# Weight preparation moved from fills into visits, and eight late stores on another queue: attention followed by a SiLU layer on one core

## The chip, the core and the metric

The kernel runs on one core of a Trainium2 chip. A core has four computing engines, each with an instruction queue of its own that it works through in order: TensorE (PE, with its weight loads shown as PEld), VectorE (DVE), ScalarE (ACT) and GpSimd (POOL). SyncE (SP) computes nothing here; it issues most of the DMA transfers between the chip's main memory (HBM) and the core's memory (SBUF). Matrix products land in PSUM, which has few buffers, and some other engine must empty them. The metric is the device time of one execution in microseconds. Before the change its median is 1379.21 us over 10 runs, from 1376.03 to 1383.0.

## What is computed

```
q_n, k_n = rmsnorm(q, g_q), rmsnorm(k, g_k)         # q, k, v: (8, 12, 448, 64)
attn     = softmax(q_n @ k_n.T / sqrt(64))
x        = (attn @ v) as (8 * 448, 12 * 64)         # 3584 rows of 768
h        = x @ w_in                                 # w_in: (768, 2048)
out      = (h * sigmoid(h)) @ w_out                 # w_out: (2048, 768)
```

The inputs q, k and v are 32-bit floats; w_in and w_out come as 64-bit floats, so the kernel rounds them to 32 bits itself.

## The kernel before

**Visits and fills.** The attention part runs over 24 visits, c = 0 to 23: a visit treats four heads of one batch, and three visits finish a batch. `visit(c)` (L1212) computes the scores of c on PE (L579), takes their exponentials on ACT (L584), weighs the values on PE (L611), divides the sums of the visit before on VectorE (`divide`, L669), and at its end adds exponentials on VectorE (`add`, L625). After each visit stands `between(c)` (L1267): it transposes the queries and keys of the next visit, sums the exponentials, takes reciprocals on VectorE (L654) and spreads them by DMA (`spread`, L660 and L662).

**The fill.** Inside `between`, `fill` (L1155) is called twice. It runs matrix work of the first layer for batches that are already finished: from c = 6 on, two batches per group of six visits (`GROUP` is 6). That work is `halves_in`: for each of eight blocks, seven products of a fast multiplication scheme (the class `Seven`), each of three steps on PE (L745; a step shows as two matmul records). A product needs a PSUM buffer, of which there are two during this part, and VectorE or ACT must empty it (L704, L752, L758). In the first group a call of `fill` has 13 steps. Small pieces of work for other engines, the list `others`, are dealt out evenly among these steps: with n others, the k-th is issued when n * steps // 13 reaches k. The list `prompt` (the two reciprocals) is dealt first: one at the start, one at step 3.

**Preparing w_in.** The weights come in 24 pieces, six for each of four chunks, handled by a `Rounder`. `load` issues the DMA from SP (L75). `open` splits the words by two activations on ACT (L90, L91). `round` takes three instructions on VectorE (L113, L116, L120), one addition on GpSimd (L124), and then tries to issue two further loads, which can only go where an earlier piece of the same buffer has been rounded. When a chunk is rounded, `sum_w_in(chunk, step)` makes four sums of its quarters on VectorE (L701, L704, 768 columns each), which the products need as left operands.

Twelve pieces and the sums of chunk 0 are done beside c = 0 to 5. The others are placed by hand. `weights_in(c, half)` (L1200) returns the pieces and sums for one call of `fill`; with i = 2 * (c - 6) + half, the table `pieces_at` says how many pieces are rounded and the next ones opened there, and `sums_at` which sums are made.

**The second layer.** After the visits, `quad(q)` runs for q = 0 to 6 over 512 rows of the output each, again with the fast scheme, on two levels. `results[i, j]` holds the two tiles (128 rows by 384 columns each) of the upper (i = 1) or lower (i = 2) rows and the left (j = 1) or right (j = 2) columns. `save_out(q, i, j)` (L1075) stores them by `store` (L442), which cuts a tile where the order of the output's rows asks for it and issues each piece at L451 from SP unless other queues are named. In the last quad the final product is stored by quarters, on the queues of ACT and SP in turn (L1135 to L1139).

**After all of it** the engines meet at closing semaphores (L1543).

Of the kernel before, what the change touches and what calls it, by code (L numbers as in the profile page):

```python
# [441 lines left out]
def store(nc, out, z, column, o, m0, *queues):  # L442


    at, queues = 0, queues or [nc.sync]
    while at < o.shape[0]:
        b, c = divmod(column + at, z.S)
        j, p = divmod(c, z.R)
        n = min(z.R - p, o.shape[0] - at)
        rows = out[ds(b * z.S, z.S), ds(m0, o.shape[1])].rearrange("(p j) m -> j p m", j=z.J)  # L450
        queues[0].dma_start(rows[j, ds(p, n)], o[ds(at, n), :])  # L451
        queues = queues[1:] + queues[:1]
        at += n
# [3 lines left out]
def bounded(  # L457
# [3 lines left out]
    P, D, R, J, S = z.P, z.D, z.R, z.J, z.S  # L461
# [9 lines left out]
    GROUP = z.NPAIR  # L471
# [10 lines left out]
    work = mem.tile([P, 16 * S + z.NK], F32, name="work")  # L482
    at = 0

    def piece(n):
        nonlocal at
        at += n
        return work[:, at - n : at]
# [6 lines left out]
    r = [piece(S) for _ in range(2)]  # L495
# [37 lines left out]
    def x_of(c, i):  # L533
        b, cp = divmod(c, z.NPAIR // 2)
        return xT(b, 2 * cp + i)
# [34 lines left out]
    def scores(c, j, i=None):  # L570


        two = ps.tile([P, 2, BANK], F32, name="sc", bufs=2)
        for half in range(2):
            pair = half if j == LEFT else i
            keys = kT[:, ds((z.KA, z.KB)[0 if j == LEFT else i] + j * P, P)]
            for h in range(2):
                rows = ds(h * D, D)
                nc.tensor.matmul(  # L579
                    two[ds(half * D, D), h, 0:S], keys[rows, ts(half, D)], qT[rows, pair, :],  # L580
                    start=True, stop=True,
                )
        for h in range(2):
            nc.scalar.activation(  # L584
                eleft[:, h] if j == LEFT else weights(c, j)[:, i, h], two[:, h, 0:S], AF.Exp,
                scale=norm.column(c, i, h, j),
            )
# [28 lines left out]
    def add(c, j):  # L616

        def one(i):
            total = weights(c, 0)[:, i]
            if j == LEFT:  # L620
                rows = ds(i * D, D)
                total, more = total[rows], eleft[rows]
            else:
                more = weights(c, j)[:, i]
            nc.vector.tensor_tensor(out=total, in0=total, in1=more, op=ALU.add)  # L625

        return [lambda: one(0), lambda: one(1)]
# [38 lines left out]
    def divide(c, source):  # L666
        for i in range(2):
            x = x_of(c, i)
            nc.vector.tensor_tensor(  # L669
                out=x, in0=x if source is None else source[i], in1=r[i], op=ALU.mult  # L670
            )

    def normalise(c):


        if c >= NC:
            return []

        def piece(name, i):
            t = scratch[i if c < GROUP + 2 else 0]  # L680
            source = raw_q[c % 2] if c < GROUP else q_of(c)
            if name == "q":
                norm.squares_q(c, source, t, i)
            else:
                norm.squares_k(c, place[f"k{c % 2}"], t, i)
            if name == "q" and c < GROUP:
                norm.root(c, name, i)
                norm.scale(c, source, q_of(c), i, nc.gpsimd)
                if i == 1 and c + 2 < GROUP:
                    load_q(c + 2)  # L690
            elif i == 1:
                norm.root(c, name)
                if name == "q":
                    for m in range(2):
                        norm.scale(c, source, q_of(c), m, nc.gpsimd)

        return [lambda a=a: piece(*a) for a in (("q", 0), ("q", 1), ("k", 0), ("k", 1))]
# [8 lines left out]
    def left_sums(a11, a12, a21, a22, s1, s2, s4, steps=range(4)):  # L706

        for step in steps:
            (
                lambda: plus(a21, a22, s1),  # L710
                lambda: minus(s1, a11, s2),
                lambda: minus(a11, a21, a21),
                lambda: minus(a12, s2, s4),
            )[step]()

    def right_sums(b11, b12, b21, b22, t1, t2, t4):

        minus(b12, b11, t1)
        minus(b22, t1, t2)
        minus(b22, b12, b12)  # L720
        minus(b21, t2, t4)
# [70 lines left out]
    def sum_w_in(i, step):  # L792

        assert room.w_in.rounded >= (i + 1) * z.NW
        summed.add((i, step))
        w = room.chunk(i).rearrange("p (c m r k) -> p c m r k", c=z.NW, m=2, r=2)
        up, low = w[:, 0:HW], w[:, HW:]
        s = room.sums(i).rearrange("p (s c m k) -> p s c m k", s=3, c=HW, m=2)
        left_sums(
            up[:, :, :, 0], low[:, :, :, 0], up[:, :, :, 1], low[:, :, :, 1],  # L800
            s[:, 0], s[:, 1], s[:, 2], (step,),
        )

    def quarters(group, c):

        return [xT(b, c + up) for up in (0, HW) for b in group]

    def sums_of_x(c):
        return [sums_x[:, ts(i * HW + c, S)] for i in range(3)]

    def sum_x(group, c):
        right_sums(*quarters(group, c), *sums_of_x(c))
# [119 lines left out]
    QUADS = NT // 4  # L932
# [8 lines left out]
    def take(n, *which):  # L941

        for i in which or range(len(regions)):
            a, at = regions[i]
            if at + n <= a.shape[1]:
                regions[i][1] += n
                return a[:, ds(at, n)]
        raise AssertionError
# [8 lines left out]
    results = {(1, 1): [take(z.HALF, i) for i in (7, 5)]}  # L957
    copies = [take(QUARTER, i) for i in (0, 0, 1, 2)]
    for at in ((1, 2), (2, 1), (2, 2)):
        a = take(2 * z.HALF)  # L960
        results[at] = [a[:, ts(t, z.HALF)] for t in range(2)]
    a = take(2 * z.HALF)
# [109 lines left out]
            )  # L1072
        return o

    def save_out(q, i, j, tiles=range(2)):  # L1075
        for t in tiles:
            store(
                nc, out, z, (4 * q + 2 * (i - 1) + t) * P, results[i, j][t], (j - 1) * z.HALF
            )

    def quad(q):
# [109 lines left out]

    pieces_at = {0: 1, 1: 1, 2: 1, 3: 2, 4: 1, 5: 1, 6: 2, 7: 2, 8: 1}
    sums_at = {-6: [(0, 0)], -5: [(0, 1)], -4: [(0, 2)], -3: [(0, 3)]}
    for i, chunk in ((1, 1), (5, 2), (8, 3)):
        sums_at[i] = [(chunk, 0), (chunk, 1)]
        sums_at.setdefault(i if i == 5 else i + 1, []).extend([(chunk, 2), (chunk, 3)])

    def weights_in(c, half):  # L1200
        def piece():
            room.w_in.round()
            room.w_in.open()

        i = 2 * (c - GROUP) + half
        work = [piece] * (1 if c < GROUP else pieces_at.get(i, 0))
        return work + [lambda a=a: sum_w_in(*a) for a in sums_at.get(i, ())]

    def last_two(c):
        return [c // GROUP * 2 - 2, c // GROUP * 2 - 1]  # L1210

    def visit(c):  # L1212

        beside = normalise(c + 1) if c <= GROUP else []
        if c < NC:
            scores(c, 0, 0)
        run_all(beside[0:1])
        if c > 0:
            weigh(c - 1, LEFT)
            weigh(c - 1, LEFT - 1, 0)  # L1220
        if c < NC:
            scores(c, 0, 1)
        if not 0 < c < GROUP:
            run_all(beside[1:2])
        if c > 0:
            weigh(c - 1, LEFT - 1, 1)
            if c - 1 < EARLY:
                for i in range(2):
                    nc.vector.tensor_copy(x_of(c - 1, i), sums[i])
                if inverting:  # L1230
                    if c > 1:
                        divide(c - 2, None)
                    run_all(inverting)
                    inverting.clear()
            else:
                divide(c - 1, sums)
                if c < NC and c % GROUP == 0:
                    for i in range(0 if c == GROUP else 1, HW):
                        sum_x(last_two(c), i)
            if c < GROUP:  # L1240
                run_all(beside[1:2])
            if c + 1 < NC:
                loads["vrest"](c + 1)
        if c == NC:
            return
        scores(c, 1, 0)
        scores(c, 1, 1)
        if c < GROUP:
            run_all(beside[2:3])
        weigh(c, 0, 1)  # L1250
        scores(c, 2, 0)
        if c < GROUP:
            run_all(beside[3:4])
        weigh(c, 1, 1)
        scores(c, 2, 1)
        weigh(c, 0, 0)
        run_all(add(c, 1))
        weigh(c, 1, 0)
        scores(c, LEFT)
        if c + 1 < NC:  # L1260
            loads["v"](c + 1)

    def run_all(work):
        for piece in work:
            piece()
# [282 lines left out]
```

## Time and profile before

| what | value |
|---|---|
| median of 10 runs | 1379.21 us |
| the profiled execution, its own time | 1378.12 us |
| its span, from the first instruction to the last | 1376.3 us |
| VectorE's part in rounding w_in, one piece: L113, L116, L120 (median of each where nothing disturbs it) | 0.42, 0.43, 0.69 us |
| a w_in sum (L701, median) | 0.95 us |
| GpSimd's addition of one piece (L124, median) | 1.29 us |
| a reciprocal, half of the columns (L654) | 1.55 us |
| the first group, c = 6 to 11 | from 134.39 to 355.00 us |
| the last instructions on VectorE and the last stores' issues | 1371.3 to 1372.1 us |

A row of the profile's timeline gives the start, the duration, the engine, the source line and operation, the tiles as "written <- read", the shapes and a count where equal rows are merged. In square brackets stands the idle time before it and what ended that. "SPq" and "ACTq" mark DMA issues. A table by stage gives, for a stretch from A to B, its length and then each engine's busy time with its number of instructions.

### The profile page before, as it was taken

The numbers are of one execution on the slowest core, as the hardware profiler recorded it, in microseconds if no ns is written. First come the engines' busy times: TensorE is split into PE (matmuls) and PEld (weight loads), VectorE is DVE, ScalarE is ACT, GpSimd is POOL, SyncE is SP. The second block draws the span as 40 slices with busy tenths as digits, with TensorE's granted clock in tenths as the row PEclk, the third lists the DMA queues.
The fourth block names the chain that finished last, engine by engine and source line by source line (L and its number), as shares of the span: only waits on it lengthen the run. The fifth ranks groups of instructions, "written<-read, shape, count | busy, mean of one in ns | idle before, by whom it ended". The sixth has DMA issues, their size and how long they took to land.

```text
span 1376.3 us, 19392 instructions
## 1 busy us (share of the span) xinstructions
PE 1335.1 (97%) x7185; PEld 817.8 (59%) x7185; DVE 888.3 (65%) x1497; ACT 517.9 (38%) x882; POOL 338.3 (25%) x233
## 2 busy tenths in 40 slices
PE   7998999999999999999999999999999999999998
PEld 4333444444444444444444455555998989898988
DVE  3887976665644544644543677667876676777775
ACT  6875555655545544545554244420000000000000
POOL 4774443332332233223320144420000000000000
PEclk9999999999999999999999999999999999999999
DMA  7654444323222322322221248421423232322321
GB/s 181 187 156 103 112 129 139 98 78 98 77 71 77 105 78 77 105 78 73 69 86 41 98 141 270 163 96 43 126 73 96 74 96 73 101 83 92 105 65 37
DMA packets 175692, 139.40 MB, mean 101 GB/s; under 512 B 104036, under 2 KB 159716, under 8 KB 175588
## 3 DMA queue, kind: packets, MB, share of 16 engines
q1 hardware_dynamic: 175264, 137.86, 34.1%
q8 instruction: 59, 0.97, 0.3%
q14 instruction: 45, 0.37, 0.1%
q10 hardware_dynamic: 324, 0.20, 0.1%
HBM read 88.47 MB, written 41.29 MB: 94 GB/s over the span
## 4 chain that ended last, share of the span: by engine, by line
PE 88%; DVE 6%; ACT 2%; issue 2%; SPq 1%; DMA 0%; POOL 0%; DVEq 0%; ACTq 0%
PE mm L745 27%; PE alone L1037 25%; PE av L611 9%; PE mm L1069 8%; PE sc L579 8%; PE alone L745 7%; DVE work L654 2%; PE sc L546 1%; PE sc L561 1%; PE sc L645 1%; PE mm L645 1%; ACT work L584 1%; DVE work L625 1%; DVE rms L396 1%; DVE W L116 1%
## 5 line engine op out<-in xcount | busy, mean ns | idle before, releaser
L745 PE MATMUL mm<-x,W 128*128 128x448 f32 x636 | 255.9, 546 | 10.7 <-DVE stage L704 7.4
L584 ACT ACTIVATE work<-sc,rms 128x448 f32<-128x448 f32 x324 | 184.3, 632 | 85.8 <-PE sc L579 77.4
L424 POOL TENSOR_TENSOR rms<-rms,minus_half 128x14 f32<-128x14 f32 (+4 forms) x55 | 138.5, 2521 | 250.4 <-DVE rms L420 194.8
L745 PEld LDWEIGHTS mm<-x,W 128*128 128x128 f32 x636 | 118.2, 191 | 134.1 <-issue 105.9
L745 PE MATMUL mm<-sums_x,W 128*128 128x448 f32 x456 | 183.4, 542 | 2.3 <-DVE stage L704 1.5
L625 DVE TENSOR_TENSOR work<-work 128x896 f32<-128x896 f32 (+1 forms) x114 | 123.4, 1116 | 77.2 <-ACT work L584 75.2
L579 PE MATMUL sc<-work 64*64 64x448 f32 x1344 | 164.3, 546 | 6.5 <-ACT work L584 4.7
L611 PE MATMUL av<-work,rows 64*64 64x448 f32 x1296 | 153.5, 547 | 7.8 <-issue 2.4
L745 PEld LDWEIGHTS mm<-sums_x,W 128*128 128x128 f32 x456 | 85.2, 190 | 88.4 <-issue 79.6
L611 PEld LDWEIGHTS av<-work,rows 64*64 64x64 f32 x1296 | 51.8, 133 | 95.8 <-issue 85.7
L579 PEld LDWEIGHTS sc<-work 64*64 64x64 f32 x1344 | 52.2, 133 | 88.8 <-issue 35.9
L1037 PE MATMUL alone<-W,rows 128*128 128x192 f32 x552 | 103.1, 326 | 0.0
L396 DVE TENSOR_REDUCE rms<-squares 112x8 f32<-112x512 f32 (+1 forms) x80 | 52.4, 655 | 64.3 <-ACT squares L395 63.4
L1037 PEld LDWEIGHTS alone<-W,rows 128*128 128x128 f32 x552 | 92.0, 190 | 0.0
L1069 PE MATMUL mm<-W,work 128*128 128x384 f32 x264 | 88.7, 486 | 0.0
L1037 PE MATMUL alone<-W,work 128*128 128x192 f32 x468 | 88.2, 326 | 0.0
L760 POOL TENSOR_TENSOR parts<-parts,stage 128x448 f32<-128x448 f32 x31 | 42.6, 1373 | 168.2 <-DVE parts L704 168.1
L1037 PEld LDWEIGHTS alone<-W,work 128*128 128x128 f32 x468 | 78.1, 190 | 0.0
L1047 ACT COPY work<-alone 128x192 f32<-128x192 f32 x38 | 12.1, 319 | 165.4 <-PE alone L1037 138.1
L1069 PEld LDWEIGHTS mm<-W,work 128*128 128x128 f32 x264 | 50.2, 190 | 35.0
L878 ACT ACTIVATE stage<-stage 128x896 f32<-128x896 f32 x63 | 57.2, 945 | 25.8 <-DVE stage L704 25.2
L395 ACT ACTIVATE squares<-rows 128x512 f32<-128x512 f32 (+1 forms) x74 | 44.8, 606 | 57.8 <-DVE rms L396 56.7
(190 smaller groups left out, 1917.2 us busy)
## 6 DMA issues: line engine op xcount, KB each, us to landing
hidden<-stage SPq DMA_DIRECT2D x63, 448.0 KB, 2.8
work<-hidden SPq DMA_DIRECT2D x21, 1024.0 KB, 5.5
rows<-in_moe_w_out_dram SPq DMA_DIRECT2D x32, 384.0 KB, 3.2
W<-in_moe_w_in_dram SPq DMA_DIRECT2D x22, 512.0 KB, 4.7
rows<-in_k_dram SPq DMA_DIRECT2D x48, 192.0 KB, 3.0
work<-work SPq DMA_DIRECT2D x144, 56.0 KB, 1.9
rows<-in_q_dram SPq DMA_DIRECT2D x36, 224.0 KB, 3.6
x<-hidden SPq DMA_DIRECT2D x7, 1024.0 KB, 5.8
```

Of the source, the lines that this page charges most:

```text
L395: nc.scalar.activation(t, rows, AF.Square)
L396: nc.vector.tensor_reduce(out=out, in_=t.rearrange("p (n d) -> p n d", n=n), axis=AX.X, op=ALU.add)
L424: nc.gpsimd.tensor_tensor(out=t, in0=t, in1=half, op=ALU.pow)
L579: nc.tensor.matmul(two[ds(half * D, D), h, 0:S], keys[rows, ts(half, D)], qT[rows, pair, :], start=True, stop=True,)
L584: nc.scalar.activation(eleft[:, h] if j == LEFT else weights(c, j)[:, i, h], two[:, h, 0:S], AF.Exp, scale=norm.column(c, i, h, j),)
L611: nc.tensor.matmul(sums[i][ds(h * D, D), :], v, w, start=(j == 0 and step == 1), stop=(j == LEFT - 1 and step == 1),)
L625: nc.vector.tensor_tensor(out=total, in0=total, in1=more, op=ALU.add)
L745: nc.tensor.matmul(t, self.left(name, s), self.right(name, s), start=s == ends[0], stop=s == ends[1])
L760: nc.gpsimd.tensor_tensor(out=u2, in0=u2, in1=p5, op=ALU.add)
L878: nc.scalar.activation(t, t, AF.Silu)
L1037: nc.tensor.matmul(t, x[:, i], y, start=i == ORDER[0], stop=i == ORDER[-1])
L1069: nc.tensor.matmul(o, a[:, 2 * i + m, t], right_one(name, i)[:, m], start=n == 0, stop=n == len(steps) - 1,)
```

## The change

Three things are done.

- The tables of `weights_in` are written out anew. `halves` gives for each call of `fill` a string of steps, "r" for a rounding and "o" for an opening, each now an element of its own in the list that is dealt. From i = 4 on an opening stands ahead of the rounding.
- A new function `weights_in_visit(c)` is called inside `visit(c)`, behind `divide` of the visit before and ahead of the loads of the values' rest. It makes the four sums of chunk 1 in visit 7 and of chunk 2 in visit 9, and two roundings in each of the visits 8 and 10. These are left out of the fills.
- `save_out` names GpSimd's queue for the last quad's lower rows (`i == 2`), and SP's as before for all others. Its unused argument `tiles` goes.

```diff
-    def save_out(q, i, j, tiles=range(2)):
-        for t in tiles:
+    def save_out(q, i, j):
+        for t in range(2):
             store(
-                nc, out, z, (4 * q + 2 * (i - 1) + t) * P, results[i, j][t], (j - 1) * z.HALF
+                nc, out, z, (4 * q + 2 * (i - 1) + t) * P, results[i, j][t], (j - 1) * z.HALF,
+                nc.gpsimd if q == QUADS - 1 and i == 2 else nc.sync,
             )
...
-    pieces_at = {0: 1, 1: 1, 2: 1, 3: 2, 4: 1, 5: 1, 6: 2, 7: 2, 8: 1}
-    sums_at = {-6: [(0, 0)], -5: [(0, 1)], -4: [(0, 2)], -3: [(0, 3)]}
-    for i, chunk in ((1, 1), (5, 2), (8, 3)):
-        sums_at[i] = [(chunk, 0), (chunk, 1)]
-        sums_at.setdefault(i if i == 5 else i + 1, []).extend([(chunk, 2), (chunk, 3)])
+    step_of = {"o": lambda: room.w_in.open(), "r": lambda: room.w_in.round()}
+    halves = {0: "ro", 1: "ro", 2: "ro", 3: "roo", 4: "or", 5: "or", 6: "or", 7: "oroo"}
+    visits = {GROUP + 2: "rr", GROUP + 4: "rr"}
+    sums_halves = {-6: [(0, 0)], -5: [(0, 1)], -4: [(0, 2)], -3: [(0, 3)]}
+    sums_halves.update({8: [(3, 0), (3, 1)], 9: [(3, 2), (3, 3)]})
+    sums_visits = {GROUP + 1: 1, GROUP + 3: 2}
 
     def weights_in(c, half):
-        def piece():
-            room.w_in.round()
-            room.w_in.open()
-
         i = 2 * (c - GROUP) + half
-        work = [piece] * (1 if c < GROUP else pieces_at.get(i, 0))
-        return work + [lambda a=a: sum_w_in(*a) for a in sums_at.get(i, ())]
+        work = [step_of[step] for step in ("ro" if c < GROUP else halves.get(i, ""))]
+        return work + [lambda a=a: sum_w_in(*a) for a in sums_halves.get(i, ())]
+
+    def weights_in_visit(c):
+        for step in visits.get(c, ""):
+            step_of[step]()
+        if c in sums_visits:
+            for step in range(4):
+                sum_w_in(sums_visits[c], step)
...
                 if c < NC and c % GROUP == 0:
                     for i in range(0 if c == GROUP else 1, HW):
                         sum_x(last_two(c), i)
+                weights_in_visit(c)
```

## The prediction

> **What bounds the kernel now.** I read four views: busy time by stage, what PE waited for, VectorE's timeline at the longest wait, and the queues' timelines at the end.
>
> First, busy time by stage: the three groups of six visits (c = 6 to 11, 12 to 17, 18 to 23), and then the gap inside four visits of the first group between the end of `divide` and the start of `add`.
>
> ```profile
> PE 1335.1 (97%) x7185; PEld 817.8 (59%) x7185; DVE 888.3 (65%) x1497; ACT 517.9 (38%) x882; POOL 338.3 (25%) x233
> ...
> 134.39:355.00 220.61, 208.17 (x1146) 94.51 (x1138) 154.38 (x207) 122.47 (x192) 90.24 (x57) 1.00 0.38 109
> 355.00:570.18 215.18, 212.14 (x1150) 98.41 (x1146) 109.66 (x148) 109.76 (x172) 66.69 (x41) 1.00 0.30 83
> 570.18:784.00 213.82, 211.06 (x1127) 97.32 (x1123) 105.12 (x137) 102.44 (x159) 52.68 (x34) 1.00 0.24 71
> ...
> 176.60:181.43 4.83, 4.71 (x48) 2.00 (x46) 0.01 (x1) 4.17 (x8) 1.58 (x2) 1.00 0.19 43
> 213.00:217.86 4.86, 4.74 (x48) 1.97 (x46) 0.01 (x1) 4.18 (x8) 0.65 (x1) 1.00 0.18 40
> 249.95:255.26 5.31, 5.12 (x56) 2.02 (x56) 0.01 (x2) 4.57 (x9) 2.39 (x3) 1.00 0.17 39
> 286.87:291.72 4.85, 4.70 (x48) 1.99 (x46) 0.00 (x1) 4.16 (x8) 0.00 (x0) 1.00 0.18 40
> ```
>
> After the stretch's length the columns are PE, PEld, DVE, ACT and POOL busy us, clock, DMA share and GB/s. PE is the bound (97%, full clock). In the first group it is idle for 220.61 - 208.17 = 12.4 us, in the others for 3.0 and 2.8: about 9.5 us can be won there. In the fills, outside these gaps, VectorE is near its limit (c = 7, from 184.10 to 209.00: 22.8 us busy of 24.9), while it stands still in the gaps: 19.85 us in the four visits.
>
> Second, what PE waited for in that group (us in total, times, longest), and VectorE at the longest wait:
>
> ```profile
> PE mm L745 <- DVE stage L704: 6.2, 7, 2.6
> PE mm L745 <- DVE parts L704: 1.6, 2, 0.9
> PE av L611 <- DVE x L669: 1.0, 1, 1.0
> ...
> 234.56 1.52 DVE L120 SCALAR_TENSOR_TENSOR W<-W 128x512 int32<-128x512 int32 x1
> 236.00 1.54 DVE L654 RECIPROCAL work<-sc 128x224 f32<-128x224 f32 x1
> 237.47 1.65 DVE L704 TENSOR_TENSOR W<-W 128x768 f32<-128x768 f32 x1
> 239.04 0.61 DVE L704 TENSOR_TENSOR stage<-mm,parts 128x448 f32<-128x448 f32 x1
> ...
> 239.70 4.78 PE L745 MATMUL mm<-x,W 128*128 128x448 f32 x12 [2.65 <-DVE stage L704]
> ```
>
> A product takes six matmul records, 2.25 us, and there are two PSUM buffers, so VectorE must empty one (L704, 0.6 us) before the second product after it. Here a rounding step, a reciprocal and a w_in sum stand in front of that emptying, and PE waits 2.65 us.
>
> Third, the end:
>
> ```profile
> 1368.76 1.28 SPq L451 DMA_DIRECT2D out_dram<-work  x1
> ...
> 1371.34 0.36 DVE L704 TENSOR_TENSOR work<-x,work 128x192 f32<-128x192 f32 x1
> ...
> 1371.72 0.32 SPq L451 DMA_DIRECT2D out_dram<-work  x1
> ...
> 1371.72 0.39 ACTq L451 DMA_DIRECT2D out_dram<-work  x1
> ...
> out_dram<-work ACTq DMA_DIRECT2D x1, 36.0 KB, 3.0
> ```
>
> VectorE's last sum ends at 1371.70, both queues issue the last stores 0.02 us later, these land 3.0 us on, and 1.6 us of closing semaphores make the span. SP was late in the middle (the L1138 store of the first quarter goes out at 1368.76 on SP, its partner on ACT at 1367.21), but has caught up for the last pair.
>
> **The change, part by part.**
>
> *Work moved into visits.* The sums of chunks 1 and 2 (eight at 0.95 us, the L701 row's median) go to visits 7 and 9; four roundings (L113 0.42 + L116 0.43 + L120 0.69 = 1.54 us) go two each to visits 8 and 10. In all 7.6 + 6.2 = 13.8 us of VectorE leave the fills. Each visit gets 3.8 or 3.1 us, behind `divide`, into a gap of 4.8 to 5.3 us: uncontended, all is hidden. What is queued behind it is only `add` (L625), whose first half frees `eleft` for the last two exponentials. `add` starts at 217.86, they at 219.33, and `add` takes 1.09: 0.4 us of room over the gap.
>
> Here a rule and a row differ. The Trainium skill ("SBUF — State Buffer", Who interferes with whom) says that a VectorE instruction with two SBUF inputs, or in a two-port mode, and a GpSimd one that reads SBUF exclude each other. The row that bears on it: in c = 7 a rounding beside two POOL additions took 1.25, 1.24 and 1.50 us in place of 0.42, 0.43 and 0.69, 2.45 us more. In visits 8 and 10 the second rounding runs beside the POOL addition (L124, 1.29 us) of the first. By the lock it waits that one instruction out: at most 1.3 us, 4.4 in all, inside the gap. By the row, 3.1 + 2.45 = 5.5 us: 0.7 over the gap, 0.3 past the slack. ACT's 0.43 us idle before L752 then takes it. I count nothing, and 0.5 us a visit (2 us in all) as the bad end.
>
> *The moved steps' other instructions.* A rounding also issues POOL's L124 and w_in loads. POOL's scaling (L439) for the next transposition is in front of it, so nobody needs POOL sooner. Three loads (pieces 18 to 20) go out in visit 8. In the SP queue two wait for POOL, and behind them stand the vrest and v loads, not needed before the next visit. Visit 10 issues none. The opens stay in the fills, but for steps 4 to 7 "open" comes before "round" of the same piece. By the dealing rule round follows one or two matmul steps (0.75 us each) after its open; the two activations take 1.31 us. ACT is free there in before (silu ends at 225.35, its next evacuation is at 228.52) and runs ahead of PE. Cost between 0 and 1 us at each of four places; I take 1.0 in all, since VectorE's backlog covers most.
>
> *Waits of PE by place:* from the timelines, before and what I expect.
> - Visit and fill c = 6: 1.02, 0.72, 0.87. The causes are `sum_x`, `add` and a reciprocal with a rounding that stays. Nothing goes.
> - c = 7: 0.62 (reciprocal late behind a sum) and 1.11 (second rounding). Both go: 1.73.
> - c = 8: 2.65. The sums are gone and the rounding is dealt at step 7, behind the evacuation, not at step 2. What is late next is the reciprocal alone, which later groups absorb. Goes: 2.65.
> - c = 9: 0.18, 0.23, and 1.19 behind two roundings in a row, of which one is left. Goes: 1.6.
> - c = 10: 0.53, behind a sum that waited for POOL's addition of the last piece; goes. 0.81 (ACT) and 0.30 stay.
> Sum: 1.73 + 2.65 + 1.6 + 0.53 = 6.5 us, less 1.0 for opens: **5.5 us**. Later stages are PE bound (busy 24.20 of 24.20 us in the fill of c = 11), so it arrives whole.
>
> *Eight stores on GpSimd's queue.* Of the last quad the tiles of its lower rows, both halves, are cut into eight transfers, all moved from SP. SP's time for them is 0.3 to 0.4 us each, but no last store waits for SP, as shown. The gain is at most the last landing's excess, 3.0 - 1.9 (the shortest) = 1.1 us, if a thinner SP queue lands sooner. No row shows a DMA from POOL. The nearest row, SP's, would give 0. The rule speaks against: the skill ("DMA: Bandwidth & Descriptors", Issuing engines are not separate DMA queues) says that more issuers save only issue time, and its Latency section puts GpSimd's first byte at about 1 us against 0.6, for software emission. Estimate from that page: at 1.1 us an issue, two go at 1363.9 to 1366.1 and six more until 1372.7; with a landing of 2 us the last is there at 1374.7, exactly where the end is now. At 2 us an issue: 1363.9 + 16 + 2 = 1381.9, 7 us later. Ends: -1.1 and +7. I take +0.5, near the SP row but with the first use of this path in the kernel against it.
>
> **Sum** against the profiled execution: 1378.1 (span 1376.3 + 1.8 around it) - 5.5 + 0.5 = 1373.1. The median is 1.1 us above that execution, so **1374.2 us**.
>
> **Rivals.**
> 1. *The stores set the end.* Emission on POOL is slow: from about 2.2 us an issue (17.6 us from 1363.9, plus 2, is 1383.5, 8.8 later) less 5.5 the kernel is slower by 3.3: 1382.5. For it: no POOL store is in the trace, and all eight stand in one queue. Against: the transfers are small (16 to 112 rows), and most of the 2 us would have to be paid each time. Chance 0.13.
> 2. *The waits only shift.* The reciprocals stay, the new open-before-round order lets VectorE wait for ACT, and only the 2.65 goes, less 0.45 of new waits: 1379.2 - 2.2 + 0.5 = 1377.5. For it: c = 6 shows waits with no sum near. Against: later groups, with the same reciprocals, show none. Chance 0.17.
> 3. *The cover in the visits is gone.* Contended roundings and sums push `add`, the exponentials and the next queries' copy by 1 us in four visits, taking 4 of the 5.5: 1378.2. Against: a 4.8 us gap for 3.1 to 3.8 us. Chance 0.06.
> Forecast, with the tail between -1 and +2: 0.64.
>
> **Numbers.** The forecast's own range is 1371.5 to 1376.5. To leave out no more than 0.2 the range reaches to cases 2 and 3 and to issues of about 1.8 us: 1371 to 1379.5. About 0.2% (2.8 us) can be told from no change. Faster: nearly all of the forecast, a little of 2: 0.65. Within: most of 2 and 3 and half-slow stores: 0.21. Slower: rival 1: 0.14.
>
> **What would show it.** PE's idle time in the first group falls from 12.4 to about 7, the 2.65 and both 1.1 us waits being gone; VectorE's gaps in visits 7 to 10 are filled and `add` is not later against the exponentials. At the end, POOL's issues: if they are done by 1372 on the old scale, the tail is as now. The prediction is wrong if the last landing comes from POOL's queue, or if VectorE waits for L91 in c = 8 and 9.

## The result and the profile after

The changed kernel takes 1371.06 us (median of 9 runs, 1368.24 to 1371.97), beside 1378.87 us for the kernel before (31 runs): a ratio of 0.9942 with a 95% interval of 0.9932 to 0.9951, 7.8 us less. The forecast was 1374.2 us, 5.0 less than the median it started from. The sign is right, the gain is about one and a half times as large as forecast, and the time lies just below the forecast's own range of 1371.5 to 1376.5 us and just inside the wide one, which begins at 1371.

The busy time by stage, first and second group of six visits, with the columns as before (length, PE, PEld, DVE, ACT, POOL, clock, DMA share, GB/s):

```profile
135.56:348.02 212.46, 207.19 (x1146) 94.78 (x1138) 153.84 (x207) 122.46 (x193) 90.84 (x57) 1.00 0.40 113
348.02:563.11 215.09, 212.13 (x1150) 98.41 (x1146) 109.66 (x148) 109.74 (x171) 66.68 (x41) 1.00 0.30 83
```

The first group takes 212.46 us in place of 220.61: 8.15 less, where the prediction had 5.5. The second is as it was. PE's idle time in the first group falls from 12.4 to 5.3 us; VectorE's work is the same (153.8 against 154.4), it only stands elsewhere. What PE still waits for there:

```profile
PE mm L745 <- DVE parts L704: 1.5, 3, 0.7
PE av L611 <- DVE x L669: 1.0, 1, 1.0
PE av L611 <- issue: 1.0, 5, 0.2
PE mm L745 <- ACT stage L758: 0.6, 1, 0.6
```

The 6.2 us behind "DVE stage" are gone, and so are the 0.8 us that had been put down to ACT's L752, which the view of before lists as:

```profile
PE mm L745 <- ACT stage L752: 0.8, 1, 0.8
```

VectorE and PE at the place of the former 2.65 us (c = 8), from their timelines:

```profile
232.43 1.55 DVE L654 RECIPROCAL work<-sc 128x224 f32<-128x224 f32 x1
233.90 0.56 DVE L704 TENSOR_TENSOR parts<-mm,parts 128x448 f32<-128x448 f32 x1
234.38 1.55 DVE L654 RECIPROCAL work<-sc 128x224 f32<-128x224 f32 x1
236.31 0.62 DVE L704 TENSOR_TENSOR stage<-mm,parts 128x448 f32<-128x448 f32 x1 [0.39 <-POOL parts L760]
...
234.51 2.52 PE L745 MATMUL mm<-sums_x,W 128*128 128x448 f32 x6 [0.23 <-DVE parts L704]
236.99 3.46 PE L745 MATMUL mm<-x,W 128*128 128x448 f32 x8
```

Between the two reciprocals stands only an emptying; VectorE even waits for POOL before the next one. PE loses 0.23 us.

The end, from the timeline, with the time to landing of two stores from the DMA view:

```profile
1357.10 0.70 POOL L451 DMA_DIRECT2D out_dram<-x  x1 [449.75 <-DVE x L704]
...
1361.24 1.02 POOL L451 DMA_DIRECT2D out_dram<-work  x2
...
1364.66 0.32 SPq L451 DMA_DIRECT2D out_dram<-work  x1
1364.66 0.39 ACTq L451 DMA_DIRECT2D out_dram<-work  x1
...
out_dram<-work ACTq DMA_DIRECT2D x1, 36.0 KB, 2.7
...
out_dram<-work POOLq DMA_DIRECT2D x1, 24.0 KB, 4.5
```

POOL issues a store in 0.5 us, the first in 0.7, and is through with all eight at 1362.3, before the last stores of SP and ACT are even due. The last landing is 2.7 us behind its issue, at 1367.4, and it is ACT's, not POOL's. From PE's last matmul to the end it is 6.55 us, 5.68 before.

Account of the two profiled spans, 1376.32 and 1370.13: the first group -8.15, the end +0.87, the stretch from c = 12 to PE's last matmul -0.08, and everything ahead of the first group +1.17. The last lies ahead of anything that was changed: a stretch at half clock at 18 us lasts 6.8 us in this run and 3.4 in the other. With it set aside the spans differ by 7.4 us, near the 7.8 between the medians. The first group by itself repeats to 0.01 us where no such stretch falls into it (220.61 before, 220.62 in a second kernel with that part as before), so the experiments are read by it.

### The profile page after: what moved, and what is told of

It is laid out like the page before. It is cut to its first block, busy times and chain, and to the rows that moved or that the text cites. A ratio compares the mean times of both kernels' runs of the same rounds, so it can differ in the third digit from the quotient of the medians.

```text
span 1370.1 us, 19386 instructions
## 1 busy us (share of the span) xinstructions
PE 1335.6 (97%) x7185; PEld 818.8 (60%) x7185; DVE 887.0 (65%) x1497; ACT 517.8 (38%) x882; POOL 342.9 (25%) x241
## 4 chain that ended last, share of the span: by engine, by line
PE 90%; DVE 4%; ACT 2%; issue 2%; DMA 1%; SPq 1%; DVEq 0%; ACTq 0%
PE mm L745 28%; PE alone L1037 25%; PE av L611 9%; PE mm L1069 8%; PE sc L579 8%; PE alone L745 7%; PE sc L546 1%; PE sc L561 1%; PE sc L645 1%; DVE work L654 1%; PE mm L645 1%; ACT work L584 1%; DVE work L625 1%; DVE rms L396 1%; DMA rows<-in_k_dram 0%
## 5 line engine op out<-in xcount | busy, mean ns | idle before, releaser
L611 PE MATMUL av<-work,rows 64*64 64x448 f32 x1296 | 153.8, 549 | 7.8 <-issue 2.5
L396 DVE TENSOR_REDUCE rms<-squares 112x8 f32<-112x512 f32 (+1 forms) x80 | 52.4, 656 | 73.5 <-ACT squares L395 72.7
```

What stands on the lines that cost most here:

```text
L396: nc.vector.tensor_reduce(out=out, in_=t.rearrange("p (n d) -> p n d", n=n), axis=AX.X, op=ALU.add)
L611: nc.tensor.matmul(sums[i][ds(h * D, D), :], v, w, start=(j == 0 and step == 1), stop=(j == LEFT - 1 and step == 1),)
```

## The experiments

All are read by the first group's time (from the first exponential of c = 6 to that of c = 12) and, where timed, by the ratio to before. Five things are at stake: which part of the change brings the gain, and whether the prediction's terms for openings, for c = 10, for cover in the visits and for the stores are right.

| kernel | first group, us | end, us | ratio, 95% interval |
|---|---|---|---|
| before | 220.61 | 5.68 | 1 |
| changed | 212.46 | 6.55 | 0.9942 (0.9932 to 0.9951) |
| e1, moved work alone | 212.17 | 6.24 | 0.9931 (0.9918 to 0.9945) |
| e2, stores alone | 220.62 | 6.68 | 1.0003 (0.9994 to 1.0013) |
| e3, sums alone | 217.27 | 6.15 | 0.9967 (0.9956 to 0.9978) |
| e4, roundings alone | 216.60 | 6.19 | 0.9964 (0.9953 to 0.9976) |
| e5, all in visit 8 | 215.46 | 5.83 | 0.9961 (0.9946 to 0.9976) |
| e6, sums over x early | 214.14 | 6.04 | 0.9963 (0.9949 to 0.9976) |
| e7, more on POOL | 212.40 | 6.59 | 0.9947 (0.9932 to 0.9962) |
| e8, open then round | 212.41 | 6.04 | 0.9931 (0.9913 to 0.9948) |
| e9, rounding of c = 6 late | 213.21 | 6.08 | 0.9953 (0.9939 to 0.9966) |
| e10, last rounding alone | 218.36 | 5.95 | one run |
| e11, e4 once more | 216.44 | 6.17 | one run |
| e12, e5 once more | 215.44 | 5.90 | one run |

### The parts: e1 and e2

e1 is the changed kernel with `save_out` on SP's queue again; e2 is the kernel before with only these lines:

```diff
+                nc.gpsimd if q == QUADS - 1 and i == 2 else nc.sync,
```

> The moved roundings and sums alone, all stores on SP as before the change. If the stores on GpSimd's queue cost about 0.9 us, as the tail of the profile suggests (5.7 us from PE's last matmul to the end before, 6.6 after), this is 0.9 us below the changed kernel, ratio to before 0.9935. If the stores bring part of the gain, it is 1 to 2 us above it, ratio 0.995 to 0.996.

> The eight stores on GpSimd's queue alone. If they cost: 0.5 to 1.1 us above before, ratio 1.0004 to 1.0008, with about 6.6 us from PE's last matmul to the end. If they bring what the forecast missed (2.8 us): ratio 0.998. If the longer end of the changed kernel's profile was chance: ratio 1.000 and 5.7 us.

The moved work is all of the gain: e1 is at 0.9931 and its first group at 212.17 us, e2 leaves the group alone and is at 1.0003. The stores bring nothing. Do they cost? In eleven profiles with the eight stores on SP the end takes 5.68 to 6.24 us, 6.02 on average; in the three with POOL 6.55, 6.59 and 6.68. That is 0.6 us, and the forecast had 0.5. About 0.3 us of it can be read off: at the close SyncE waits for 12 semaphore pairs in a row in place of 8, 0.06 us each, and from the first of these waits to the end of the span it is 1.64 us in the changed kernel and in e2, and 1.34 to 1.36 in the eleven others. In the timed runs it can't be told: the intervals of e1 and the changed kernel overlap, and that of e2 holds 1.

### Sums or roundings: e3, e4 and e11

e3 keeps the old list of pieces and moves the sums; e4 (run again as e11) keeps the sums in the fills:

```diff
-    sums_visits = {GROUP + 1: 1, GROUP + 3: 2}
+    sums_visits = {}
+    sums_halves.update({1: [(1, 0), (1, 1)], 2: [(1, 2), (1, 3)], 5: [(2, s) for s in range(4)]})
```

> Only the eight sums moved (7.6 us of VectorE), roundings and openings as before, stores on SP. Theory of the place (a wait is made by what stands in front of one emptying): the 2.65 us of c = 8 fall to about 1, since the rounding is still between the two reciprocals; 1.1 and 1.2 us behind two roundings in a row stay; gain 2 to 2.5 us, ratio 0.998. Theory of the load (each us taken off VectorE's fills counts alike, 8.15 us for 13.8): gain 4.5 us, ratio 0.9967.

> Only four roundings moved (6.2 us of VectorE) with the new order of openings, sums as before, stores on SP. Theory of the place: the waits behind two roundings in a row (1.1 and 1.2 us), 0.4 and 0.5 us go, and part of the 2.65 us; gain 3.5 to 4.5 us, ratio 0.997. Theory of the load: 3.6 us, ratio 0.9974. Both parts together give 8.15 us in the profile; if the two alone add up to clearly less, they share waits that only go when both are gone.

> The roundings alone once more (the kernel of e4_rounds_only): in its profile a 3.4 us stretch at half clock fell into c = 8, whose period came out 2.2 us longer than before. Without such a stretch in the first group it should take 216.6 less about 1.7: 214.5 to 215.2 us. If the 2.2 us belong to the kernel: 216.6 again.

The sums bring 3.3 us in the first group, more than the "theory of the place" had given them (2 to 2.5) and less than the theory of the load (4.5); the timed ratio, 0.9967, is the one that the latter named. So the size doesn't decide between them. The waits do. PE's waits behind "DVE stage" in the first group of e3:

```profile
PE mm L745 <- DVE stage L704: 3.6, 6, 1.2
```

The wait of 2.65 us has fallen to nothing, not to 1, and the other waits (1.1, 1.2, 0.5, 0.8, 0.3) are all still there, as the theory of the place says and the theory of the load does not. The roundings bring 4.0 us, but with a flaw that came back in e11. PE's timeline of e11, and its busy time in a stretch at that place:

```profile
239.76 6.47 PE L745 MATMUL mm<-x,W 128*128 128x448 f32 x12 [2.11 <-DVE stage L704]
...
240.60:244.00 3.40, 3.40 (x6) 1.64 (x5) 3.37 (x5) 0.14 (x1) 0.00 (x0) 0.50 0.56 169
```

The sums left in the fill make PE wait 2.1 us, and for the next 3.4 us its clock is at 0.50: twelve matmul records take 6.47 us, where before they took 4.78. In e4 the same wait, at 236.47, was followed by a half-clock stretch from 237.3 on. Of the two alternatives for e11 the second came out, 216.4 us: the stretch came again, behind the wait. What the roundings would bring without it was not measured; the half-clock stretch costs about 6.47 - 4.78 = 1.7 us. For the same reason 3.3 and 4.0 us, beside the 8.4 of e1, don't show whether the two parts share a wait.

### Does an opening just ahead of its rounding cost? e8

```diff
-        work = [step_of[step] for step in ("ro" if c < GROUP else halves.get(i, ""))]
+        joined = {4: ["or"], 5: ["or"], 6: ["or"], 7: ["or", "o", "o"]}
+        steps = ["ro"] if c < GROUP else joined.get(i, halves.get(i, ""))
+        work = [lambda s=s: [step_of[a]() for a in s] for s in steps]
```

> As e1_visits_only, but for steps 4 to 7 open and round are one element, so that a rounding is issued straight behind its opening, with no matrix step between. If VectorE really waits for ACT in this order (the 1.0 us of the prediction), its waits for L91 appear, up to 1.3 us each at four places, and the group is 0.5 to 2 us longer than e1's 212.2. If ACT runs far ahead of VectorE anyway, no waits and the same time.

The group takes 212.41 us, 0.2 more than e1. All of VectorE's waits in this kernel from 200 to 280 us, which holds c = 8 and 9:

```profile
DVE rms L396 <- ACT squares L395: 8.6, 5, 3.5
DVE x L669 <- PE av L611: 8.3, 3, 3.6
DVE stage L704 <- POOL parts L760: 2.4, 2, 2.0
DVE stage L704 <- PE mm L745: 1.8, 2, 1.4
DVE parts L704 <- PE mm L745: 1.8, 2, 1.0
DVE work L625 <- ACT work L584: 1.0, 2, 0.6
DVE stage L704 <- issue: 0.3, 1, 0.3
```

There is no wait for L91, although nothing at all stands between the openings and their roundings in the program: ACT ends L91 0.9 to 3.1 us before VectorE starts the L113 of the same piece. VectorE's waits in the first group of the changed kernel name no L91 either. The 1.0 us that the prediction took off for the openings was zero.

### The waits of c = 10: e10

The kernel before, with one rounding moved and nothing else:

```diff
-    pieces_at = {0: 1, 1: 1, 2: 1, 3: 2, 4: 1, 5: 1, 6: 2, 7: 2, 8: 1}
+    pieces_at = {0: 1, 1: 1, 2: 1, 3: 2, 4: 1, 5: 1, 6: 2, 7: 2}
...
+                if c == GROUP + 4:
+                    room.w_in.round()
```

> The kernel before with one thing moved: the 24th piece is rounded in visit 10 and no longer in the fill behind it; everything else, the stores and the sums too, as before. If the three waits of c = 10 (0.53, 0.81, 0.30 us) are one chain behind VectorE's 1.4 us for POOL's addition of that piece, all three go, and the first group takes 218.3 to 218.9 us in place of 220.62. If 0.81 (put down to ACT) and 0.30 (to a sum) are waits of their own, as the prediction had them, only 0.5 goes: 220.1.

One rounding of 1.54 us brings 2.26 us. PE's three waits of c = 10 in the kernel before:

```profile
306.08 2.52 PE L745 MATMUL mm<-x,W 128*128 128x448 f32 x6 [0.53 <-DVE stage L704]
309.41 2.52 PE L745 MATMUL mm<-sums_x,W 128*128 128x448 f32 x6 [0.81 <-ACT stage L752]
312.24 2.52 PE L745 MATMUL mm<-sums_x,W 128*128 128x448 f32 x6 [0.30 <-DVE stage L704]
```

VectorE's timeline of the kernel before, and below it that of e10:

```profile
302.44 0.69 DVE L120 SCALAR_TENSOR_TENSOR W<-W 128x512 int32<-128x512 int32 x1
304.53 0.96 DVE L704 TENSOR_TENSOR W<-W 128x768 f32<-128x768 f32 x1 [1.40 <-POOL W L124]
305.41 0.62 DVE L704 TENSOR_TENSOR stage<-mm,parts 128x448 f32<-128x448 f32 x1
```

```profile
300.63 0.62 DVE L704 TENSOR_TENSOR stage<-mm,parts 128x448 f32<-128x448 f32 x1
301.17 1.23 DVE L704 TENSOR_TENSOR W<-W 128x768 f32<-128x768 f32 x1
302.44 0.96 DVE L701 TENSOR_TENSOR W<-W 128x768 f32<-128x768 f32 x1
303.32 0.62 DVE L704 TENSOR_TENSOR stage<-mm,parts 128x448 f32<-128x448 f32 x1
```

Before, the sum of the last chunk came straight behind the last rounding and had to wait 1.40 us for POOL's addition. So the emptying behind it was 2 us late (305.41 against 303.32). In e10 PE waits for nothing in the fill of c = 10: with the 0.53 us, the 0.81 put down to ACT's L752 and the 0.30 put down to VectorE go as well. So they were one delay handed on. The timelines fit a way through L396, which ACT's squares wait for (ACT's L752 starts at 308.84 before and at 305.88 in e10), and through the reciprocals.

### Is the gap in the visits really the limit? e5 and e12

```diff
-    sums_visits = {GROUP + 1: 1, GROUP + 3: 2}
+    sums_visits = {GROUP + 1: 1, GROUP + 2: 2}
```

> As e1_visits_only, but the four sums of chunk 2 in visit 8 too, behind its two roundings: about 7 us of VectorE and 1 us of contention in a gap of 4.9. If a visit's cover is what keeps PE running: add is some 3 us late, the last exponentials with it, and the group loses 1 to 3 us against e1's 212.2. If PE has other work to go on with (it runs matrix steps of the fill behind the visit), nothing: 212 +/- 0.3.

> Sums and roundings both in visit 8 once more (the kernel of e5_both_in_visit8), whose profile had a stretch at half clock in c = 8 as well. If the overflow itself costs: about 2 us over e1's 212.17, with PE waiting about 2 us for ACT's L752. If it was the clock alone: 212.3.

It is. VectorE's timeline of e12 behind `divide` of visit 8, and then PE:

```profile
215.66 0.69 DVE L120 SCALAR_TENSOR_TENSOR W<-W 128x512 int32<-128x512 int32 x1
217.76 0.96 DVE L704 TENSOR_TENSOR W<-W 128x768 f32<-128x768 f32 x1 [1.40 <-POOL W L124]
218.75 2.69 DVE L701 TENSOR_TENSOR W<-W 128x768 f32<-128x768 f32 x3
221.36 5.08 DVE L625 TENSOR_TENSOR work<-work 128x896 f32<-128x896 f32 x5
...
224.98 5.35 PE L745 MATMUL mm<-sums_x,W 128*128 128x448 f32 x9 [1.97 <-ACT stage L752]
```

`add` starts at 221.36, 4.4 us later against `divide` than in the changed kernel (217.34 there, with `divide` 0.4 us later). The exponentials that it releases are late, then ACT's evacuation behind them, and PE waits 1.97 us, again with 3.4 us at half clock directly behind. Both profiles give 3.3 us over e1, a little more than the 1 to 3 expected: 2.0 us of it are PE's idle time (7.0 in place of 5.0 in e5), and 1.3 its busy time, with the half-clock stretch in it. The first alternative held; "PE has other work to go on with" did not.

### Two attempts at the rest: e6 and e9

Of the waits that remain, 0.72 and 0.52 us stand in c = 6. e6 makes a third of the sums over x earlier, e9 moves one rounding to c = 7, both on top of e1:

```diff
                 begun[0] = fetch_ahead([0, 1], 0)
+                sum_x([0, 1], 0)
```

```diff
-    halves = {0: "ro", 1: "ro", 2: "ro", 3: "roo", 4: "or", 5: "or", 6: "or", 7: "oroo"}
+    halves = {1: "ro", 2: "roro", 3: "roo", 4: "or", 5: "or", 6: "or", 7: "oroo"}
```

> As e1_visits_only, but the first third of the sums over x for the first group made at the end of the work beside c = 5, not in visit 6. Theory: of the 2.9 us that PE still waits in this group, 0.72 and 0.52 stand behind sums over x and add in visit 6, and go: 1.2 us less than e1, ratio 0.9922. The 1.0 us (PE to VectorE and back) stays. Rival: VectorE is as full at the end of c = 5, and PE waits there instead: no difference, or 1 us more.

> As e1_visits_only, but the first rounding and opening of c = 6 moved to the first fill of c = 7, where VectorE has room since the sums are gone. If the 0.52 us at c = 6 stands behind that rounding: the first group takes 211.6 us (e1: 212.17), ratio 0.9927. If c = 7 is still too full for two roundings in one fill: a wait of 1 us there, 212.7.

Both lose, e9 by the group's time alone, since its timed interval overlaps that of e1. In e6 the two waits are gone, but `divide` in visit 6 comes later, and PE's waits in the group read:

```profile
PE av L611 <- DVE x L669: 3.1, 1, 3.1
PE av L611 <- issue: 1.1, 6, 0.2
PE mm L745 <- ACT stage L758: 0.6, 1, 0.6
```

The 1.0 us of e1 has become 3.1, with a half-clock stretch behind it. In e9 the 0.52 us goes and 0.81 and 0.82 us appear in c = 7 and 8. In e6 the loss is at another place than the rival had it: behind `divide` of visit 6, since the sums in front of it start it 2.1 us later in the group, and not at the end of c = 5. In e9 the rival is what happened, with two waits in place of one.

### A double dose on POOL: e7

The changed kernel with SP's last four quarter stores on GpSimd's queue too.

```diff
-                    z.HALF + h * QUARTER, *((nc.scalar, nc.sync)[:: 1 if h else -1]),
+                    z.HALF + h * QUARTER, *((nc.scalar, nc.gpsimd)[:: 1 if h else -1]),
```

> The changed kernel with SP's four last quarter stores on GpSimd's queue as well. If an issue on POOL costs what the profile shows (0.5 us against 0.32 to 0.47 on SP) and its landing is alike, the end is the same, 6.6 us from PE's last matmul, ratio 0.994. If a store on that path is slower[...], 0.5 to 1.5 us longer.

The end takes 6.59 us, as in the changed kernel. Twelve stores cost no more than eight, so the 0.6 us isn't a price for each store.

## Why the prediction was right in kind and short in size

**The mechanism.** PE bound, stalled in the first group by what stands in front of an emptying on VectorE, and a gap in the visits that takes the work: e1, e3 and e10 show it. The rivals fall: the stores don't set the end (POOL issues in 0.5 us, not 2.2); the waits didn't only shift (7.2 us of PE's idle time are gone); the cover in the visits held, as far as PE is concerned.

**The step that failed is the sum of PE's waits by place**, 6.5 us less 1.0:

- "Less 1.0 for opens": measured 0 (e8).
- "0.81 (ACT) and 0.30 stay" in c = 10: both went, 1.1 us, since they were one chain with the 0.53 (e10). The prediction took the releaser's name, ACT, for the cause, without asking what ACT itself had waited for.
- c = 6, "nothing goes": 0.87 became 0.51, 0.36 us. It is 0.52 in e4 and 0.87 in e3, so it comes with the new order of roundings and openings.
- c = 7, "both go": only the 1.11 went. The 0.62 is still there, and stands in all fourteen profiles, so the sum that the prediction blamed didn't make it. In c = 8, 0.23 is left of the 2.65.

So 6.5 + 1.1 + 0.36 - 0.62 - 0.23 = 7.1 us of idle time, and 12.44 - 5.27 = 7.2 is measured. The errors have both signs: the two over-counts hid 0.85 us of what the others had left out. The remaining 1.0 of the 8.15 us had no term at all: PE's busy time fell too, from 208.17 to 207.19 us for the same 1146 matmul records. A record lasts 0.54 us, but in a run of them one follows the other after 2.25 / 6 = 0.375 us; the last one before a wait counts its whole length as busy. So each wait costs some 0.16 us more than its idle time (an estimate from these two figures), and some six fewer gaps, 20 in place of 26, make the 1.0 us. In e10, where three waits go, the busy time falls by 0.6 us. That is worked out from the traces, not tried by itself.

**Cover in the visits.** The prediction allowed at most 2.45 us of contention per visit with roundings and nothing on the path. VectorE in visit 10 of the changed kernel, with POOL's instructions below:

```profile
281.85 0.43 DVE L116 TENSOR_SCALAR W<-W 128x512 int32<-128x512 int32 x1
282.31 1.41 DVE L120 SCALAR_TENSOR_TENSOR W<-W 128x512 int32<-128x512 int32 x1
283.65 2.51 DVE L113 TENSOR_SCALAR W<-W 128x512 f32<-128x512 f32 x1
286.19 0.43 DVE L116 TENSOR_SCALAR W<-W 128x512 int32<-128x512 int32 x1
...
281.94 2.68 POOL L439 TENSOR_TENSOR rows<-rows,rms 112x512 f32<-112x512 f32 x2
284.59 1.28 POOL L124 TENSOR_TENSOR W<-W 128x512 int32<-128x512 int32 x1
```

L113 takes 2.51 us in place of 0.42: it ends just behind POOL's first L124, so it seems to have waited two POOL instructions out, where the prediction had taken one from the lock that the Trainium skill ("SBUF — State Buffer", Who interferes with whom) describes. The row of c = 7, where each instruction took about 0.8 us more, gives a similar total: here 0.72 + 2.09 = 2.8 us. In visit 8 `add` still starts 4.85 us behind `divide`, as before, but its first instruction takes 1.74 us in place of 1.09 while POOL's second L124 runs; in visit 10 it starts 0.9 us later. The last exponentials, which had 1.48 and 1.46 us of idle time in front of them before, now wait 1.85 and 1.73 us for it. So the sign "`add` is not later" holds in visit 8 and fails in visit 10, but PE waits for none of it. Some microseconds more cost, as e5 shows.

**The end.** +0.5 forecast, +0.6 measured by the profiles. The estimate of 1.1 us an issue was twice too high, and the place of the cost is another: neither the emission nor the landings. From PE's last matmul to the last landing it is 3.8 to 4.7 us in the three kernels with POOL and 4.0 to 5.1 in the eleven others. What is longer is the close behind it, and of that only the 0.3 us for four more semaphore pairs are identified. The sign "done by 1372 on the old scale" came true (1362.3, which is 1369.3 there), but the tail was not "as now". That the size was nearly met is luck.

**No kernel tried beats the changed one beyond doubt.** e1 and e8, with the stores left on SP, come out lower by 0.0011, inside the intervals.

## What to carry to other kernels

When one engine is the bound in a stage and another has to empty its buffers, work on the second is priced by what it stands in front of, not by its length: one rounding of 1.5 us in front of a wait for a third engine cost 2.3 us, and 13.8 us moved into gaps brought 8.2. Before a wait is set down as one that stays, follow its releaser back: three waits with three names in c = 10 were one delay. And measure the gap that is to take the work with all its contention, since an `add` 4.4 us late cost 3.3 us in e5, more than the 2.65 us wait of c = 8.

## What was not expected of the hardware

A wait of PE of 2 to 3 us can be followed by 3.4 us at half clock, at some 1.7 us of time. It was so behind the waits of e4 and e11 (2.1 us), e5 and e12 (1.97) and e6 (3.07), each time within about 1 us of the wait's end; the 2.65 us in the profiles of the kernel before, of e2 and of e10 were not followed by one. All kernels here share a wait of 2.73 us in c = 4, which shows both cases: ten of the fourteen profiles have a stretch at half clock there, and four have none. PE's timeline, and two stretches of 3.41 us, first before, then e3:

```profile
109.02 3.35 PE L745 MATMUL mm<-x,W 128*128 128x448 f32 x4 [2.73 <-DVE stage L704]
...
105.64:109.05 3.41, 0.68 (x3) 0.03 (x1) 3.34 (x6) 0.25 (x1) 0.48 (x1) 1.00 0.83 226
109.05:112.46 3.41, 3.41 (x8) 1.30 (x12) 3.09 (x2) 0.00 (x0) 0.80 (x1) 0.50 0.34 135
```

```profile
109.54 1.77 PE L745 MATMUL mm<-x,W 128*128 128x448 f32 x4 [2.73 <-DVE stage L704]
...
105.21:108.62 3.41, 1.60 (x10) 0.30 (x2) 2.62 (x4) 1.19 (x3) 0.00 (x0) 1.00 0.90 248
108.62:112.03 3.41, 2.49 (x12) 1.04 (x16) 3.41 (x4) 0.00 (x0) 1.28 (x1) 1.00 0.46 163
```

The same wait; four records then take 3.35 us at clock 0.50 in the one and 1.77 at 1.00 in the other, and c = 4 takes 25.3 and 23.6 us. What differs is where the wait falls on a grid of time. Within one profile the half-clock stretches start whole multiples of 3.413 us apart (at 20.30 and 109.05 in the kernel before, 26 times; at 18.82 and 237.27 in e4, 64 times). On this grid, the kernel before has 3.41 - 0.68 = 2.73 us of idle time within one window; in e3 the wait is divided between two windows, with 3.41 - 1.60 = 1.81 us in the first. All fourteen profiles, from 8 to 1360 us, agree: each of the 29 windows at full clock with 1.89 us of idle time or more is followed by one at half clock, and none with 1.81 us or less is. The 2.65 us of c = 8 was divided in each of its three profiles, with at most 1.7 us in one window. The Trainium skill ("TensorE: Matmul & The Clock Gate", Part 1) has such a window, 3413 ns long and free-running; its limit for idle gaps, about 3 us (same page, "Why this matters for your kernels"), is not what these traces show.

Two things follow. Such stretches, one more or one fewer, go with the spread between runs of one kernel: of the runs of the kernel before, one of 1375.12 us has a mean clock of 1.000, and one of 1382.72 us has 0.993. And whether runs of the kernel before with a mean clock of 0.993 to 0.994 met one behind the 2.65 us wait, so that its removal brings part of the timed gain, stays open: those runs have no trace.
